# A recurrent attention layer with a gated MLP on one core: a new order table, no tensor arithmetic on GpSimd, and r and v loaded in two transfers without zero rows

## The chip, the cores and the metric

The kernel runs on one core of one Trainium2 chip. A core has five engines that run side by side, each through its own list of instructions in the order in which they were written: TensorE (PE in the profile; PEld are its weight loads), VectorE (DVE), ScalarE (ACT), GpSimd (POOL) and SyncE (SP), which here issues all DMA transfers. They wait for each other through semaphores. The metric is the device time of one execution in microseconds; the number to predict is the median over several runs.

## What is computed

For 32 heads (batch 4 times 8) of size 40, a state of 40x40 is carried through 768 time steps. The outputs of all heads are put side by side, 3072 tokens of 320 numbers, and go through an MLP of width 2048 with the gate h * erf(softplus(h)).

```python
for t in range(S):
    y[:, :, t] = np.einsum('bhd,bhde->bhe', rt, state)
    Sa = np.einsum('bhde,bhe->bhd', state, at)
    state_decay = state * wt[:, :, None, :] - np.einsum('bhd,bhe->bhde', Sa, bt)
    state = state_decay + np.einsum('bhd,bhe->bhde', vt, kt)
...
    h = x @ w_in
    sp = np.maximum(h, 0.0) + np.log1p(np.exp(-np.abs(h)))
    g = h * erf(sp)
    return (g @ w_out).astype(np.float32)
```

## The kernel before

The heads are worked in two groups of 16, the 768 time steps in blocks of 128 (a block is called q here, 12 in all) and these in steps of 32 (48 in all). Names in the profile are those of tiles.

**Before a block's steps.** `prep` scans the decays w (Wt, Pr). `aphase`, once per step, scales k and b (tile bk, L672) and a (tile Ab, L667), sends Ab to the ring Zs by DMA, multiplies them on TensorE (pA, L677), masks the product into Zs (L684), sends part of it to a scratch tensor AD in memory, and transposes bk (L695). `tphase`, once per block, reads AD back as Ti, inverts small triangular matrices there on VectorE (28 short instructions that depend on each other, L724 and L725; called the solve below), sends them out (TD) and back (Tb), transposes them (T, L733) and finishes the inverse with two passes of 128 tiny matmuls on TensorE (L740).

**A step of the chain.** The state MT is copied to Zm; TensorE forms Z (L785) from Zm and Zs; a copy zt; U (L794); a copy us; from us four copies u go into the tile Vu. In the first block these are engine copies out of PSUM; in the other eleven blocks they are four DMA transfers Vu<-Us. Us is transposed (L821) and copied into the tile vt, beside r and v that a DMA brought (vt<-in_rv_e); a product pQ (L830), masked into Vu (L833); and the product my (L841, L845) from Vu, the state and r. From my VectorE adds to the state (MT, L848) and forms the outputs (L852), which leave to a tensor xd. The next step starts from MT.

**The MLP** follows two blocks behind: per block 8 times two products into ph (L1006) and a copy h, then tanh, ln, ln, exp and gelu on ScalarE (L1014), nd, rho, E and G on VectorE (L1039, L1040, L1051, L1052), and the second product into po (L1061). nd, E, bk, Ab, xl (L990, low parts of x) and a few others may run on VectorE or on GpSimd. Weights are loaded and split into high and low parts in the first 140 us (L932 to L963).

**What sets the order.** All operations are recorded in a list with their engines. `Plan.schedule` holds a planner with costs, but it is passed over where two tables, ORDER and ENGINES, fit the list, and they do: ORDER gives the position of each operation, ENGINES its engine by a letter. A -1 in ORDER is a filler, a matmul of 512 columns on constants (L579), that keeps TensorE busy while it waits in the start. All DMA transfers go through SP's queue, one after the other, from the helper `dma` (L576); copies that may run on ScalarE or VectorE go through the helper `copy` (L571 on ScalarE, L573 on VectorE).

## Time and profile before

| | us |
|---|---|
| median of 3 runs | 861.12 (860.7 to 871.73) |
| span of the profiled execution | 855.2 |
| what lies around the span, against the median | 5.9 |
| TensorE busy | 741.9 (87%) |
| VectorE busy | 626.0 (73%) |
| ScalarE busy | 563.6 (66%) |
| GpSimd busy | 145.3 (17%) |

Busy time is the time in which an engine works on an instruction; waiting for semaphores and issuing DMAs is not in it. Fillers count as busy time of TensorE. One execution was profiled; its own time is the span and what the launch puts around it.

### The profile page before, as it was taken

To read this page: it belongs to the slowest core of one execution; us is meant where nothing else is said; L and a number is where in the kernel's file an instruction comes from. 1 tells how busy PE (TensorE), PEld (TensorE's weight loads), DVE (VectorE), ACT (ScalarE), POOL (GpSimd) and SP (SyncE) were. 2 spreads that over 40 slices of the span, in tenths; PEclk is the share of its full clock that TensorE was granted. 3 is DMA by queue.
4 is the path that set the end of the run, shared out by engine and by line. 5 is a ranking of instruction groups with operands and counts; after the bars stand their busy time and mean duration, and the time that the engine had idled before them with its cause. 6 is when DMAs were issued, how large, how long until landed. Compare 5 with 4: busy or idle time off the path is not lost.

```text
span 855.2 us, 32264 instructions
## 1 busy us (share of the span) xinstructions
PE 741.9 (87%) x13794; PEld 572.6 (67%) x13794; DVE 626.0 (73%) x1331; ACT 563.6 (66%) x1055; POOL 145.3 (17%) x124
## 2 busy tenths in 40 slices
PE   0596898798889998989888998899899999899987
PEld 0343546667767777767667776687777777677864
DVE  5588776687767787879687887768688766565764
ACT  5156424677756776865875874685685787567993
POOL 0302111102012012033030100231130240112100
PEclk9998998999999999999999999989999999899998
DMA  7756664665675755556645555746546543512100
GB/s 213 216 155 156 172 157 119 134 135 142 135 169 115 145 139 123 138 121 143 160 122 118 139 130 115 158 109 146 141 112 128 126 112 92 123 39 66 36 16 19
DMA packets 185585, 107.58 MB, mean 126 GB/s; under 512 B 134268, under 2 KB 167804, under 8 KB 185436
## 3 DMA queue, kind: packets, MB, share of 16 engines
q1 hardware_dynamic: 185436, 105.46, 51.8%
q8 instruction: 110, 1.80, 0.9%
q14 instruction: 39, 0.32, 0.1%
HBM read 83.72 MB, written 14.16 MB: 114 GB/s over the span
## 4 chain that ended last, share of the span: by engine, by line
PE 43%; DMA 21%; DVE 14%; SPq 8%; ACT 6%; issue 6%; POOL 1%; DVEq 0%; ACTq 0%; POOLq 0%
PE po L1061 15%; PE ph L1006 10%; SPq L576 8%; DMA Zs<-Ab 3%; PE pA L740 3%; DMA Ti<-AD 3%; PE ph L579 3%; DMA Tb<-TD 2%; PE my L841 2%; PE pQ L830 2%; PE pA L677 2%; DMA bk<-in_kba_e 2%; DMA AD<-Zs 2%; DVE h L1052 2%; PE my L794 2%
## 5 line engine op out<-in xcount | busy, mean ns | idle before, releaser
L1061 PE MATMUL po<-wo,h 128*128 128x320 f32 x768 | 255.1, 459 | 6.1 <-DVE h L1052 5.8
L1061 PEld LDWEIGHTS po<-wo,h 128*128 128x128 f32 x768 | 135.7, 195 | 51.4 <-DVE h L1052 8.7
L1014 ACT ACTIVATE l<-l 128x512 f32<-128x512 f32 x192 | 112.0, 625 | 18.2 <-DVE nd L1039 14.4
L1006 PE MATMUL ph<-xh,wih 128*128 128x256 f32 x384 | 96.1, 332 | 3.4 <-ACT h L571 3.4
L1006 PE MATMUL ph<-xh,wil 128*128 128x256 f32 x384 | 78.0, 285 | 0.0
L1006 PE MATMUL ph<-xl,wih 128*128 128x256 f32 x384 | 77.7, 284 | 0.0
L1052 DVE SCALAR_TENSOR_TENSOR h<-l,h 128x512 f32<-128x512 f32 x96 | 70.3, 739 | 3.0 <-POOL l L1051 2.1
L1040 DVE SCALAR_TENSOR_TENSOR r<-nd,r 128x512 f32<-128x512 f32 x96 | 68.1, 709 | 5.9 <-POOL nd L1039 4.8
L1039 POOL TENSOR_TENSOR nd<-l,r 128x512 f32<-128x512 f32 x27 | 35.7, 1321 | 206.9 <-DVE r L1040 120.4
L1006 PEld LDWEIGHTS ph<-xh,wih 128*128 128x128 f32 x384 | 61.3, 194 | 10.2 <-ACT h L571 4.3
L571 ACT COPY Zm<-MT 40x320 f32<-40x320 f32 x71 | 32.4, 457 | 50.5 <-DVE MT L848 45.6
L579 PE MATMUL ph<-d 104*128 104x512 bf16 x257 | 65.7, 407 | 0.0
L1051 POOL TENSOR_TENSOR l<-l,r 128x512 f32<-128x512 f32 x27 | 38.2, 1419 | 158.6 <-ACT l L1014 85.8
L1006 PEld LDWEIGHTS ph<-xh,wil 128*128 128x128 f32 x384 | 60.6, 194 | 3.9 <-issue 3.9
L1014 ACT ACTIVATE l<-h 128x512 f32<-128x512 f32 x96 | 57.2, 628 | 7.2 <-DVE h L573 6.0
L1006 PEld LDWEIGHTS ph<-xl,wih 128*128 128x128 f32 x384 | 60.2, 192 | 0.0
L1039 DVE TENSOR_TENSOR nd<-l,r 128x512 f32<-128x512 f32 x69 | 49.7, 721 | 11.6 <-ACT r L1014 9.5
L1006 PE MATMUL ph<-xl,wir 128*128 128x256 f32 x192 | 54.9, 286 | 3.8 <-issue 3.7
L841 PE MATMUL my<-Vu,sg 64*40 64x72 f32 x1536 | 48.5, 233 | 8.7 <-DVE h L1052 3.1
L1014 ACT ACTIVATE r<-r 128x512 f32<-128x512 f32 x96 | 55.2, 624 | 0.4
L1014 ACT ACTIVATE r<-l 128x512 f32<-128x512 f32 x96 | 54.2, 619 | 1.5 <-DVE l L1051 1.4
L1006 PE MATMUL ph<-xh,wir 128*128 128x256 f32 x192 | 54.8, 285 | 0.0
(137 smaller groups left out, 1472.5 us busy)
## 6 DMA issues: line engine op xcount, KB each, us to landing
vt<-in_rv_e SPq DMA_DIRECT2D x48, 416.0 KB
bk<-in_kba_e SPq DMA_DIRECT2D x45, 416.0 KB
wo<-in_moe_w_in SPq DMA_DIRECT2D x10, 512.0 KB
h<-in_moe_w_out SPq DMA_DIRECT2D x10, 512.0 KB
Pr<-in_w_e SPq DMA_DIRECT2D x12, 419.7 KB
Rt<-in_r_e SPq DMA_DIRECT2D x48, 104.0 KB
Vu<-in_v_x SPq DMA_DIRECT2D x96, 40.0 KB
Zm<-in_v_s SPq DMA_DIRECT2D x48, 80.0 KB
```

The costliest lines, as they stand in the source:

```text
L571: self.nc.scalar.copy(o, i)
L576: self.P.add(name, "SP", lambda e: self.nc.sync.dma_start(o(), i()), rd, wr, pr, ISSUE.get(name, 0.41))
L579: self.nc.tensor.matmul((self.ph[1], self.pQ)[x], self.d1[:, :128], self.d1[:, :512], start=True, stop=True)
L740: nc.tensor.matmul(pw[js, i], l[js, i], r[js, i], start=True, stop=True)
L841: nc.tensor.matmul(my[h * 64:h * 64 + 40, x, j], sg[xs, j, h], vu[xs, j // 2 * 2 + h, j % 2], start=True, stop=False)
L1006: nc.tensor.matmul(ph[:, j * 256:j * 256 + 256], a[:k, fs], b[:k], start=(m == 0), stop=(m == 7))
L1014: self.P.add(name, "ACT", lambda e: nc.scalar.activation(out=o, in_=i, **kw), rd, wr + ["act"], pr, 0.62)
L1039: P.add("nd", [("DVE", 0.69), ("POOL", 1.28)], lambda e, r=r, l=l, nd=nd: s.eng(e).tensor_tensor(out=nd, in0=l, in1=r, op=ALU.mult), [("l" ...
L1040: P.add("rho", "DVE", lambda e, r=r, nd=nd: nc.vector.scalar_tensor_tensor(out=r, in0=nd, scalar=2 * C4, in1=r, op0=ALU.add, op1=ALU.mult) ...
L1051: P.add("E", [("POOL", 1.28), ("DVE", 0.69)], lambda e: s.eng(e).tensor_tensor(out=l, in0=l, in1=r, op=ALU.mult), [("r", ir)], [("l", il)] ...
L1052: P.add("G", "DVE", lambda e: nc.vector.scalar_tensor_tensor(out=h, in0=l, scalar=-1.0, in1=h, op0=ALU.add, op1=ALU.mult), [("l", il)], [( ...
L1061: nc.tensor.matmul(po, h[:, bs], s.wo[:, f], start=(f == 0), stop=(f == 15))
```

## The change

Both tables are new. The planner is gone; where the tables do not fit, operations now run in the order in which they were recorded (this concerns a fallback path that this input does not enter). No operation of arithmetic may run on GpSimd any more. The list of operations differs in two places: r and v come by two transfers of 40 rows and 3 KB a row, one for each half, instead of one of 104 rows and 4 KB a row, in which rows 40 to 63 and half of r's places were zero; the tile vt is cleared once in the start. And the four copies u read us in all blocks and may run on ScalarE, VectorE or as a DMA: by the new table 106 of the 192 run on ScalarE, 37 on VectorE and 49 as DMAs (before: 11, 5 and 176). A DMA may be issued from GpSimd's queue, but the new table lets SP issue all of them: 828, before 907. The fillers number 124, before 257. The b and k of the block's fourth step in the start go to the ring bk instead of the second vt tile.

```diff
-ORDER = (
-    7, 11, 13, 12, 17, 16, 144, 6, 135, 18, 5, 15, 19, 3, 126, 136, 349, 129, 10, 130, 4, 20, 8, 23, 41, 162, 0, 137, 147, 138, 139, 22, 140, 24, 21,
...
+ORDER = tuple(int(x) for x in """
+20 7 18 22 16 354 355 10 13 9 3 128 8 23 15 11 17 4 131 21 25 0 132 129 6 130 155 27 133 12 134 28 137 146 138 156 26 157 135 30 31 1 32 43 149 35 147 139 55 24 36 38 160 140 37
...
     def dma(self, name, o, i, rd=(), wr=(), pr=0):
-        self.P.add(name, "SP", lambda e: self.nc.sync.dma_start(o(), i()), rd, wr, pr, ISSUE.get(name, 0.41))
+        q = {"SP": self.nc.sync, "POOLQ": self.nc.gpsimd}
+        self.P.add(name, [("SP", ISSUE.get(name, 0.41))] + [("POOLQ", 1.0)] * (name in BULK), lambda e: q[e].dma_start(o(), i()), rd, wr, pr)
...
-            P.add("nd", [("DVE", 0.69), ("POOL", 1.28)], lambda e, r=r, l=l, nd=nd: s.eng(e).tensor_tensor(out=nd, in0=l, in1=r, op=ALU.mult), [("l", il), ("r", ir)], [("nd", i_)], pr)
+            P.add("nd", [("DVE", 0.69)], lambda e, r=r, l=l, nd=nd: s.eng(e).tensor_tensor(out=nd, in0=l, in1=r, op=ALU.mult), [("l", il), ("r", ir)], [("nd", i_)], pr)
...
-        s.dma("rv", lambda: vr, lambda: I["rv_e"][g, ck].rearrange("p (a x) -> p a x", a=NP), wr=[("vt", ivt, 0), ("vt", ivt, 1)], pr=prl)
+        for h in range(2):
+            s.dma("rv", lambda h=h: vr[h * 64:h * 64 + 40, h * 256:h * 256 + 768], lambda h=h: I["rv_e"][g, ck, h], wr=[("vt", ivt, h)], pr=prl)
...
-            if q == 0:
-                P.add("zmu", [("ACT", 0.28), ("DVE", 0.32)], lambda e, uv=uv, js=js: s.copy(e, uv, pz[js]), ["pz"], [("vu", iv, "u", j)], pr)
-            else:
-                s.dma("zu", lambda uv=uv: uv, lambda js=js: uo[js], [("us", iu, "-")], [("vu", iv, "u", j)], pr)
+            q2 = {"SP": nc.sync.dma_start, "ACT": nc.scalar.copy, "DVE": nc.vector.tensor_copy}
+            P.add("zu", [("ACT", 0.28), ("DVE", 0.25), ("SP", 0.6)], lambda e, uv=uv, js=js: q2[e](uv, uo[js]), [("us", iu, "-")], [("vu", iv, "u", j)], pr)
```

The new tables move instructions everywhere; three places show it. First TensorE's list in the second chain step of the start, from Z (out of Zm and Zs) to U (out of zt and Tb) and what follows it. Before:

```order
L785 MATMUL my<-Zm_77,Zs_69 32x40 x16
L579 LDWEIGHTS d_113
L579 MATMUL ph_159<-d_113 128x512
L579 LDWEIGHTS d_113
L579 MATMUL ph_159<-d_113 128x512
L579 LDWEIGHTS d_113
L579 MATMUL ph_159<-d_113 128x512
L794 MATMUL my<-zt_109,Tb_83 32x40 x16
L677 MATMUL pA<-Ab_76,bk_99 64x2x32 x8
```

Now, where L592 is Z, L617 the transpose of MT, L601 U, L626 the transpose of Us, L387 a filler and L483 the product pA:

```order
L592 MATMUL my<-Zm_77,Zs_69 32x40 x16
L617 MATMUL pQ<-ident,MT 104x104 x4
L601 MATMUL my<-zt_109,Tb_83 32x40 x16
L626 MATMUL pQ<-ident,Us_85 104x128 x2
L387 LDWEIGHTS d_113
L387 MATMUL ph_159<-d_113 128x512
L483 MATMUL pA<-Ab_76,bk_99 64x2x32 x8
```

The three fillers between Z and U gave way to the transpose of the state, and the transpose of Us now follows U directly.

Second VectorE's list in the middle of the first solve (L724 and L725 on the tile Ti; L932 to L942 prepare weights). Before:

```order
L724 TENSOR_TENSOR tmp_106<-Ti 128x54
L942 TENSOR_TENSOR wil_127<-l_132,wih_125 128x512
L942 TENSOR_TENSOR wil_126<-l_136,wih_124 128x512
L937 TENSOR_TENSOR l_136<-l_135,r_138 128x512
L933 SCALAR_TENSOR_TENSOR r_139<-wo,r_139 128x512
L725 TENSOR_TENSOR Ti<-Ti,tmp_106 128x6x9
L724 TENSOR_TENSOR tmp_106<-Ti 128x56
L725 TENSOR_TENSOR Ti<-Ti,tmp_106 128x7x8
L724 TENSOR_TENSOR tmp_106<-Ti 128x56
L725 TENSOR_TENSOR Ti<-Ti,tmp_106 128x8x7
L937 TENSOR_TENSOR l_132<-l_131,r_139 128x512
```

Now, with the solve at L530 and L531 and the weights at L737 to L742:

```order
L531 TENSOR_TENSOR Ti<-Ti,tmp_106 128x4x11
L742 TENSOR_TENSOR l_132<-l_131,r_139 128x512
L530 TENSOR_TENSOR tmp_106<-Ti 128x50
L531 TENSOR_TENSOR Ti<-Ti,tmp_106 128x5x10
L530 TENSOR_TENSOR tmp_106<-Ti 128x54
L531 TENSOR_TENSOR Ti<-Ti,tmp_106 128x6x9
L737 TENSOR_SCALAR r_137<-wo 128x512
L530 TENSOR_TENSOR tmp_106<-Ti 128x56
L531 TENSOR_TENSOR Ti<-Ti,tmp_106 128x7x8
L530 TENSOR_TENSOR tmp_106<-Ti 128x56
L531 TENSOR_TENSOR Ti<-Ti,tmp_106 128x8x7
```

Before, 11 instructions of other work stand between the first and the last of the 28; now three do (two of 512 columns with two inputs, one with one).

Third SP's list around the sixth chain step. Before:

```order
L576 DMA Vu_78<-in_v_x 32x8x40
L576 DMA Vu_79<-Us_85 32x4x40 x2
L576 DMA AD_118<-Zs_70 32x8x32
L576 DMA Zm_77<-in_v_s 32x640
L576 DMA Vu_79<-Us_85 32x4x40
L576 DMA Rt_82<-in_r_e 104x256
L576 DMA Vu_78<-in_v_x 32x8x40
L576 DMA Vu_79<-Us_85 32x4x40
L576 DMA AD_118<-Zs_70 32x8x32
```

Now, with L611 for a copy u as a DMA and L384 for all others:

```order
L384 DMA vt_107<-in_rv_e 40x768
L384 DMA Zm_77<-in_v_s 32x640
L611 DMA Vu_79<-Us_85 32x4x40
L384 DMA Vu_78<-in_v_x 32x8x40
L384 DMA AD_118<-Zs_70 32x8x32
L384 DMA Vu_79<-in_v_x 32x8x40
L384 DMA AD_118<-Zs_70 32x8x32
L384 DMA Rt_82<-in_r_e 104x256
```

Of the four Vu<-Us of that step one is left in SP's list, and vt<-in_rv_e stands there twice per step.

## Rows read from the trace of the kernel before

**Rows 1.** Busy time by engine in four stretches between marks of the program: the wait for the first inverse, the first four chain steps (to the fourth MT), the 43 steps up to the 47th MT, and the end. Columns: the stretch and its length, busy time (and instructions) of PE, PEld, DVE, ACT and POOL, the granted clock of TensorE, the DMA share, GB/s.

```profile
39.70:75.60 35.90, 28.03 (x119) 12.07 (x118) 28.32 (x65) 19.13 (x37) 5.37 (x4) 0.96 0.58 143
75.60:131.30 55.70, 49.43 (x1026) 28.04 (x1026) 40.45 (x89) 23.08 (x53) 6.51 (x6) 0.96 0.71 177
131.30:777.10 645.80, 585.10 (x12066) 472.36 (x12066) 486.57 (x1052) 448.79 (x846) 115.44 (x95) 0.97 0.55 127
777.10:855.20 78.10, 69.69 (x471) 52.56 (x471) 47.17 (x85) 58.47 (x95) 9.11 (x6) 0.95 0.08 25
```

**Rows 2.** The chain of work that ended last: shares of the whole span by engine, and shares of the stretch from 131.3 to 777.1 us by line. SPq is SP issuing, a DMA's time runs from its issue to its landing.

```profile
PE 43%; DMA 21%; DVE 14%; SPq 8%; ACT 6%; issue 6%; POOL 1%; DVEq 0%; ACTq 0%; POOLq 0%
...
by line: PE po L1061 15.6%; PE ph L1006 12.4%; SPq L576 9.4%; issue 6.2%; PE pA L740 4.0%; DMA Zs<-Ab 3.8%; DMA Ti<-AD 3.5%; DMA Tb<-TD 3.3%; PE my L841 2.6%; PE pA L677 2.3%; PE pQ L830 2.2%; DMA AD<-Zs 2.0%; PE my L794 2.0%; DVE h L1052 1
```

**Rows 3.** Timeline of TensorE around a wait in the middle of the span: start and length in us, and in brackets the idle time before. The same transpose of MT (L812) stands behind the wait and 14 us later.

```profile
555.04 0.37 PE L1006 MATMUL ph<-xl,wir 128*128 128x256 f32 x1 [3.67 <-issue]
...
555.64 0.90 PE L812 MATMUL pQ<-ident,MT 104*104 104x104 f32 x4
...
570.13 0.56 PE L812 MATMUL pQ<-ident,MT 104*104 104x104 f32 x4
```

**Rows 4.** The fillers: busy time of PE and PEld by L579 alone in the first two stretches of rows 1, and two pieces of the chain of work in order of time (start, length).

```profile
39.70:75.60 35.90, 27.99 (x116) 12.04 (x116) 0.96 0.58 143
75.60:131.30 55.70, 32.09 (x126) 11.37 (x126) 0.96 0.71 177
...
107.13 1.30 PE ph L579 x6
...
108.88 1.30 PE ph L579 x6
```

**Rows 5.** Timeline of VectorE: first and last instruction of the first solve, then of the second, with pieces out of its middle.

```profile
54.15 0.17 DVE L724 TENSOR_TENSOR tmp<-Ti 128x14 f32<-128x14 f32 x1
...
66.43 0.17 DVE L725 TENSOR_TENSOR Ti<-Ti,tmp 128x14 f32<-128x14 f32 x1
...
110.12 0.17 DVE L724 TENSOR_TENSOR tmp<-Ti 128x14 f32<-128x14 f32 x1
...
113.01 0.20 DVE L725 TENSOR_TENSOR Ti<-Ti,tmp 128x44 f32<-128x44 f32 x1
113.25 0.21 DVE L724 TENSOR_TENSOR tmp<-Ti 128x50 f32<-128x50 f32 x1
...
113.51 1.25 POOL L672 TENSOR_TENSOR bk<-bk,Wt 104x512 f32<-104x512 f32 x1 [1.50 <-DMA bk<-in_kba_e]
113.74 1.09 DVE L724 TENSOR_TENSOR tmp<-Ti 128x54 f32<-128x54 f32 x1
...
119.25 0.17 DVE L725 TENSOR_TENSOR Ti<-Ti,tmp 128x14 f32<-128x14 f32 x1
```

**Rows 6.** Operations of VectorE beside GpSimd. Of two lines first the group (count | busy us, mean ns | idle before it), then the same instructions' shortest, median and longest time in ns; last GpSimd's share of a third line.

```profile
L1052 DVE SCALAR_TENSOR_TENSOR h<-l,h 128x512 f32<-128x512 f32 x96 | 70.3, 739 | 3.0 <-POOL l L1051 2.1
L1052 DVE SCALAR_TENSOR_TENSOR h<-l,h x96: 644/685/2432, 180.7 to 844.9; 128x512 f32<-128x512 f32 x96
L667 DVE TENSOR_TENSOR Ab<-bk,Pr 104x512 f32<-104x512 f32 x36 | 30.1, 835 | 14.9 <-DMA Zs<-Ab 11.7 <-DMA Vu<-Us 3.2
L667 DVE TENSOR_TENSOR Ab<-bk,Pr x36: 676/691/2492, 21.4 to 696.5; 104x512 f32<-104x512 f32 x36
L1039 POOL TENSOR_TENSOR nd<-l,r x27: 1264/1285/1787, 202.1 to 785.8; 128x512 f32<-128x512 f32 x27
```

**Rows 7.** SP's issues of three transfers (shortest, median and longest time of one issue in ns), the size of two of them, and the queue's packets, MB and share of the 16 engines.

```profile
L576 SPq DMA_DIRECT2D Vu<-Us x176: 585/605/1823, 141.2 to 784.4; - x176
L576 SPq DMA_DIRECT2D vt<-in_rv_e x48: 307/480/2112, 30.6 to 768.2; - x48
vt<-in_rv_e SPq DMA_DIRECT2D x48, 416.0 KB
Vu<-Us SPq DMA_DIRECT2D x176, 20.0 KB
q1 hardware_dynamic: 185436, 105.46, 51.8%
```

**Rows 8.** Copies: those of u out of PSUM in the first block, on ScalarE and on VectorE, and one of h on VectorE (ns as above).

```profile
L571 ACT COPY Vu<-my x11: 282/283/285, 86.7 to 124.0; 32x160 f32<-32x160 f32 x11
L573 DVE COPY Vu<-my x5: 318/329/331, 85.1 to 123.6; 32x160 f32<-32x160 f32 x5
L573 DVE COPY h<-ph x20: 651/684/693, 150.0 to 826.3; 128x512 f32<-128x512 f32 x20
```

**Rows 9.** Who TensorE waited for (us in total, times, longest us), and one wait of U for the copy zt in the timeline.

```profile
PE pA L740 <- DVE T L733: 13.4, 6, 7.9
PE pA L677 <- DVE Ab L667: 8.4, 4, 2.9
PE po L1061 <- DVE h L1052: 5.8, 5, 2.7
PE my L785 <- DMA Zm<-in_v_s: 4.6, 5, 1.5
PE my L841 <- DMA Vu<-Us: 1.6, 2, 1.2
119.87 0.37 PEld L794 LDWEIGHTS my<-zt,Tb 32*32 32x32 f32 x32 [0.42 <-ACT zt L571]
```

More of the change, by code (lines that the diff above doesn't have):

```diff
@@ L295, in add @@
             self.rd[k] = []
-        every, one = alts, self.only.get(name + self.tag, self.only.get(name))
-        alts = [x for x in every if x[0] == one] or every
-        self.ops.append(dict(name=name, tag=self.tag, alts=alts, all=every, fn=fn, deps=deps, pr=pr, banks=[k for k in rd if k in self.BANKS], uses=[k for k in self.SPARE if k in rd or k in wr]))
+        self.ops.append(dict(name=name, tag=self.tag, alts=alts, fn=fn, deps=deps, keys=set(rd) | set(wr)))
         return i
     def schedule(self):
-        ops = self.ops
@@ L303, in schedule @@
-        n = len(ops)
-        if len(self.engines) == n and sorted(x for x in self.order if x >= 0) == list(range(n)):
-            for o, e in zip(ops, self.engines):
-                o["eng"] = dict(P="PE", A="ACT", V="DVE", G="POOL", S="SP")[e]
-            out = []
-            for x in self.order:
-                if x < 0:
-                    ops.append(dict(name="warm", eng="PE", fn=lambda e, x=-1 - x: self.filler(x)))
-                    x = len(ops) - 1
-                out.append(x)
-            return out
@@ L314, in schedule @@
-        succ = [[] for _ in range(n)]
-        left = [0] * n
-        for i, o in enumerate(ops):
-            left[i] = len(o["deps"])
-            for d, raw in sorted(o["deps"]):
-                succ[d].append((i, raw))
-        ready_at = [0.0] * n
-        free = {e: 0.0 for e in self.HOP}
-        ticks = {}
-        queue = lock = 0.0
-        only = [o["alts"][0][0] if len(o["alts"]) == 1 else "" for o in ops]
-        bank = {k: ("", 0.0) for k in self.BANKS}
-        uses = {k: sum(k in o["uses"] for o in ops) for k in self.SPARE}
@@ L420, in schedule @@
-        assert done == n, (done, n)
-        self.total = max(o["end"] for o in ops)
-        return sorted(range(len(ops)), key=lambda i: (start[i], i))
+        ops, n = self.ops, len(self.ops)
+        if len(self.engines) != n or sorted(x for x in self.order if x >= 0) != list(range(n)):
+            for o in ops:
+                o["eng"] = o["alts"][0][0]
+            return list(range(n))
+        for o, e in zip(ops, self.engines):
+            o["eng"] = CODE[e]
+        out = []
+        for x in self.order:
+            if x < 0:
+                ops.append(dict(name="warm", eng="PE", fn=lambda e, x=-1 - x: self.filler(x)))
+                x = len(ops) - 1
+            out.append(x)
@@ L425, in restride @@
+        return out
 def restride(ap, dim, step):
@@ L462, in host @@
     o["r_e"] = stk(re).reshape(NG, 24, 104, NP * 32)
[L463 to L466 removed]
+    rs, vs = [el(x)[:, :, :, :, [pair(n) for n in range(NP)]] for x in (r, v)]
+    vu = np.zeros((NG, 24, 2, 40, NP, 2, 32), np.float32)
+    vu[..., 0, :] = vs
+    rv = np.zeros((NG, 24, 2, 40, 3 * NP * 32), np.float32)
+    for h in range(2):
+        rv[:, :, h, :, (256, 0)[h]:(768, 512)[h]] = vu[:, :, h].reshape(NG, 24, 40, NP * 64)
+        rv[:, :, h, :, (0, 512)[h]:(256, 768)[h]] = rs[:, :, h].reshape(NG, 24, 40, NP * 32)
+    o["rv_e"] = rv
     vs = v.reshape(NG, NB, 4, 2, 24, 32, 40).transpose(0, 4, 5, 1, 2, 3, 6)
@@ L500, in __init__ @@
         K = self.K
-        self.P = Plan(K.get("po", {}), self.warm, K.get("warm", 4.0), order=ORDER, engines=ENGINES)
+        self.P = Plan(self.warm, ORDER, ENGINES)
         pool = lambda n, **k: ctx.enter_context(tc.tile_pool(name=n, bufs=1, **k))
@@ L1158, in build @@
             mlp(q)
-        if "prs" in K:
-            for o, x in zip(N.P.ops, K["prs"]):
-                o["pr"] = x
         order = N.P.schedule()
```

222 lines of the change are left out of this document (54 added, 168 removed), and 303 rows, old and new, of the table ORDER.

## The prediction

> **What bounds the kernel now.** I read the busy time by stretch first [rows 1]. In the 43 chain steps that fill most of the span, 645.8 us, TensorE is busy for 585.1 us and idle for 60.7; VectorE is busy for 486.6 us (75%), ScalarE for 448.8 (69%). So TensorE bounds this stretch, at 91%, and an order can win there at most the idle time and what the clock loses. The four chain steps of the start are different: of TensorE's 49.4 busy us in 55.7, 32.1 are fillers [rows 1, 4], so 17.3 us are work, and the stretch goes at the speed of a chain of short steps across all engines. Next I read the chain of work that ended last [rows 2]: TensorE has 43% of the span, DMA 21%, VectorE 14%, SP's issuing 8%, ScalarE 6%, GpSimd 1%. Last the clock [rows 3]: behind an idle time of 3.67 us the same transpose takes 0.90 us that takes 0.56 us 14 us later; that is work at the lower of the two levels, 1.2 instead of 2.4 GHz. In the 43 steps the granted clock is 0.97, which at 585.1 busy us is 17.6 us lost for 60.7 us of idle time, 0.29 us for each us. Saved idle time brings that back too.
>
> **The change part by part.** I make the sum against the profiled execution's 855.2 us; the median is 5.9 us above it.
>
> *The start.* Three things. (a) The first solve runs from 54.15 to 66.60, 12.45 us, with 11 other instructions in it [rows 5]. Undisturbed, one of its 28 instructions follows the other after 0.24 us (113.01 to 113.25), 6.7 us in all; the three that are left in it cost at most 0.69 us each [rows 6], so it takes 8.8 us: minus 3.7. The weight work pushed behind it is late instead, but nothing of the MLP is asked of TensorE before the fifth chain step. (b) The second solve takes 9.3 us (110.12 to 119.42), with a piece that took 1.09 us beside a GpSimd instruction [rows 5]. Now only one update of MT stands in it: 6.7 plus about 0.5, minus 2.1. (c) From the first to the fourth step the order has 26 fillers, before 90. A filler takes 0.217 us (six in 1.30) and lies on the chain there [rows 4]; 64 of them are 13.9 us. Bounds: nothing, if the second inverse (its DMAs to memory and back) is what the next block waits for anyway, and 13.9. I take 12, near the upper end, because the rows show fillers on the chain itself. Together minus 18; at the lower bound of (c), minus 6.
>
> *Copies u.* 127 of 176 transfers Vu<-Us go, and ScalarE gets 95 copies more, VectorE 32 more. On SP an issue took 0.605 us [rows 7]: 76.8 us less, against 48 more issues of rv at 0.48, 23.0. SP's list shrinks from 907 issues to 828, 9%. In the 43 steps SP's issuing has 9.4% of the chain, 60.7 us [rows 2]; 9% of that is minus 5.3. Bounds: nothing, and 53.8 (all of it on the chain); the small share on the chain speaks for the lower end. TensorE's direct waits for these transfers sum to only 1.6 us [rows 9]; 127 of 176 of that is minus 1.2.
>
> *rv in two transfers.* Each step moves 2 x 40 x 3 KB = 240 KB instead of 416 [rows 7]: 48 x 176 KB, 8.4 MB, and with the copies u (127 x 20 KB, 2.5 MB) 10.9 of 105.5 MB, 10.4%. Nobody on the chain waits much for rv itself; what gains is what queues behind it. The four small transfers on the round trip to memory and into Zs (Zs<-Ab, Ti<-AD, Tb<-TD, AD<-Zs) have 12.6% of the chain, 81.4 us [rows 2]; 10.4% of it is minus 8.5. Bounds: nothing (their own latency), and 15.4, if all of rv, a fifth of the bytes, had stood in front of them. I take the share of the bytes. The Trainium skill speaks against this edit: "DMA: Bandwidth & Descriptors", Rules for kernel authors, says that two transfers to disjoint halves of the partitions do not pay, since they serialize on the same engines. Its section on why a DMA increments its semaphore by 16 adds that a transfer uses as many engines, up to 16, as divide its rows: 13 for 104 rows, 10 for 40. An estimate by that page: 24 KB per engine and step instead of 32, a quarter less, so that the term would be minus 5.9. No row shows the engines of one transfer.
>
> *GpSimd's arithmetic.* 115 operations move: 94 of 512 columns at 0.69 us on VectorE [rows 6], 64.9 us, and 21 smaller ones, up to 14 more; I take 73 together. In return VectorE's own operations are no longer stretched: L1052 has a mean of 739 ns against a median of 685, L667 835 against 691 [rows 6], 5.2 us each. VectorE hands 12 copies of h at 0.684 [rows 8] and some 32 smaller ones, at no less than 0.27, to ScalarE, minus 16.8, and takes 32 copies u at up to 0.329, plus 10.5. Net plus 56 us, and ScalarE gets plus 47 (95 x 0.283 [rows 8] and the copies). What hides this is idle time: in the 43 steps VectorE has 159 us free and ScalarE 197 [rows 1]. By their shares of the chain, 14% and 6% [rows 2], it costs plus 7.9 and plus 2.8. On the other side an operation that waited for GpSimd took 1.285 us there [rows 6]; GpSimd's 1% of the chain, 8.6 us, about halves: minus 4.0. Net plus 6.7; bounds minus 14 (all stretching and GpSimd's share on the chain, the new load hidden) and plus 56.
>
> *The rest of the order.* Between Z and U TensorE needs about 0.65 us of other work to cover the copy zt; with nothing between them it idles for 0.42 [rows 9]. By the order that cover is short in 18 of the last 44 steps before and in 4 now, but between U and the transpose of Us it is short more often now (7 against 2). I put nothing down for it.
>
> *Sum.* -18 - 5.3 - 1.2 - 8.5 + 6.7 = -26.3; the 15 us of terms that shorten waits in the 43 steps bring 0.29 x 15 = 4.4 us of clock back. 855.2 - 30.7 = 824.5 us, and with 5.9 us around it 830 us, 3.6% less.
>
> **Rivals.**
>
> *The waits shrink much more.* Both tables steer every wait; if the new one halves the idle time of the 43 steps (minus 30.4, with the clock minus 8.8) beside the start's minus 18, it is 855.2 - 57.2 + 5.9 = 804 us. For it: the largest waits are few and long (L740 for T 13.4 us in 6, L677 for Ab 8.4 in 4 [rows 9]), the kind that an order can remove. Against it: VectorE and ScalarE have less room than before.
>
> *The waits only change their place.* The fillers go, but the second inverse sets the start; SP's and DMA's savings end at engines that are fuller. Then the solves' 5.8 us are left: 855 us. For it: several engines are three quarters full.
>
> *TensorE runs cold in the start.* With 133 fillers fewer it idles instead, and the 17.3 us of work of the four steps run at 1.2 GHz, twice as long: 830 + 17 = 847 us. For it: rows 3. Against it: 46 fillers of that stretch remain, between the longest waits. The Trainium skill, "TensorE: Matmul & The Clock Gate", section on HAM oscillation, says the same, that bursts between idle gaps start cold; by that rule the trace agrees for gaps of some us.
>
> *VectorE becomes the bound, and it gets slower.* The place is the MLP's nd, rho, E and G: those that ran beside VectorE now stand in its one list, ahead of the masks and MT updates for which TensorE waits. Each us on the path costs 1.29 with the clock. Without the start's gain, the savings of SP, DMA and clock (19) stand against it; it is slower by over 2% once more than 28 of the 56 us lie on the path, and with three quarters of them it is 861 - 19 + 54 = 896 us. For it: G already holds TensorE up (5.8 us [rows 9]). Against it: 159 us free.
>
> **How the numbers follow.** Forecast 0.50, its own range 815 to 844; waits much shorter 0.20; waits change place 0.14; cold start 0.06; VectorE bound 0.10. A measurement of this kernel can tell about 2%, 17 us, from no change: below 844 is faster, above 878 slower. Faster 0.70 (the first two), same 0.20 (the next two), slower 0.10. The range for 8 times in 10 goes from 798, below the first rival, to 862, which takes in the two middle ones and leaves out the last.
>
> **What would show it.** In the changed profile the fourth MT update should stand near 113 us (now 131.3) and the first solve take under 9.5 us; the 43 steps 632 to 638 us, with TensorE idle under 50; SP's share of the chain under 8% of them; VectorE's mean for L1052's line within 10 ns of its median; VectorE's busy time near 680 us, ScalarE's near 610. The prediction is wrong if VectorE appears as the releaser of most of TensorE's waits, if the copies of h or tanh start later behind ScalarE's new copies, if the first four steps show matmuls of double length, or if the second inverse waits for its DMAs as long as before.

## The result, and the profile after

The changed kernel takes 784.09 us in the median (779.93 to 791.56, 4 runs), the kernel before 860.91 us beside it; the ratio is 0.9143, interval 0.9075 to 0.9211. That is 8.6% less where 3.6% were forecast, and below the forecast range; it is also below 798 us, the lower end of the range for 8 times in 10. The profiled execution spans 780.8 us (before 855.2), 74.4 us less. Its own time, 782.75 us, is 2.0 us above its span; so the 5.9 us that the forecast put around the span were mostly the distance of the profiled execution from the median.

By the marks of [rows 1], the fourth MT update stands at 110.0 us (131.3 before), the 47th at 702.5 (777.1), and the end takes 78.3 us (78.1). So the start gave 21.3 us, the 43 steps 53.3 and the end nothing. The busy time by stretch, from the last product of the first block's pA to the first inverse, to the fourth MT, to the 47th, and to the end; columns as in [rows 1]:

```profile
33.30:57.90 24.60, 11.34 (x50) 4.67 (x48) 22.34 (x61) 13.27 (x26) 0.00 (x0) 0.72 0.89 234
57.90:110.00 52.10, 41.75 (x945) 26.96 (x946) 37.20 (x88) 28.81 (x67) 0.00 (x0) 0.74 0.63 159
110.00:702.50 592.50, 571.60 (x12056) 470.69 (x12055) 506.62 (x1153) 492.79 (x967) 0.00 (x0) 0.99 0.51 123
702.50:780.80 78.30, 68.16 (x474) 52.99 (x473) 50.62 (x88) 56.65 (x93) 0.00 (x0) 0.94 0.08 24
```

In the 43 steps TensorE is idle for 592.5 - 571.6 = 20.9 us, before 60.7: 39.8 us less. Its busy time fell by 13.5 us. Of these 3.3 are fillers (5.6 us in 15 before, 2.3 us in 8 now); the other 10.2 came with a granted clock of 0.99 instead of 0.97, which is 0.26 us for each us of idle time saved, where the forecast had 0.29. VectorE is now 86% busy there and ScalarE 83%, and still TensorE waits less. In the start the clock is only 0.72 to 0.74 (0.96 before); what such a clock costs in the old order is shown by old_fewfill below. The chain that ended last, by engine over the span and by line over the 43 steps (L866 and L811 are the MLP's products, L1061 and L1006 before):

```profile
PE 75%; ACT 7%; DVE 7%; DMA 4%; issue 4%; SPq 1%; DVEq 0%; ACTq 0%
...
by line: PE po L866 30.3%; PE ph L811 25.3%; PE pA L546 5.1%; PE my L646 4.4%; PE pQ L635 4.3%; PE pA L483 3.8%; PE my L601 3.2%; issue 3.0%; PE my L592 2.9%; PE pQ L617 2.5%; PE pA L501 2.3%; PE my L650 1.8%; PE pQ L626 1.5%; ACT l L819 1.
```

Beside [rows 2], TensorE went from 43 to 75%, DMA from 21 to 4%, SP's issuing from 8 to 1%: the chain is now nearly TensorE's list alone. Whom TensorE waited for in the 43 steps (us in total, times, longest), before and after. The sums of [rows 9] are those of the whole span, so the lines of before are given for the same stretch:

```profile
PE pA L740 <- issue: 7.4, 4, 2.6
PE pA L740 <- DVE T L733: 5.5, 5, 2.2
PE pA L677 <- DVE Ab L667: 4.7, 2, 2.9
PE my L785 <- DMA Zm<-in_v_s: 4.6, 5, 1.5
PE my L794 <- issue: 4.0, 2, 3.2
```

```profile
PE pA L546 <- issue: 4.9, 3, 2.2
PE my L601 <- issue: 2.9, 3, 1.3
PE ph L811 <- issue: 2.2, 1, 2.2
PE pA L483 <- DVE nd L844: 2.0, 1, 2.0
PE pA L483 <- issue: 1.7, 2, 0.9
PE pQ L626 <- ACT Sm L378: 1.4, 1, 1.4
PE my L646 <- DMA Vu<-Us: 1.2, 1, 1.2
```

The waits for T, Ab and Zm are gone. Of the 20.9 us that are left, 11.7 are "issue", time in which TensorE waited for nothing that the profile shows; what it is stays open. Where the idle time of the 43 steps went I summed from TensorE's timeline, step by step, between the products of the chain (us over 43 steps: length of the way, idle in it; UT is the transpose of Us, and what is missing from the 60.7 and 20.9 us lies within the products):

```
             MT to Z     Z to U      U to UT    UT to pQ   pQ to my   my to MT
before     124.0 12.4   93.9 17.6   90.0 2.4   81.6 7.6   74.2 14.3   36.3 0.2
after      106.3  2.4  120.9 11.1   66.0 2.2   57.4 0.1   67.4  0.2   33.0 0.0
```

The saving is no single wait: about 10, 6, 8 and 14 us in four places. The new order also spreads TensorE's other work anew: the way from Z to U is 27 us longer, the two ways from U to pQ are 48 us shorter.

The start, VectorE's timeline (first and last instruction of each solve, to [rows 5]):

```profile
40.56 0.17 DVE L530 TENSOR_TENSOR tmp<-Ti 128x14 f32<-128x14 f32 x1 [1.19 <-DMA Ti<-AD]
...
48.09 0.19 DVE L531 TENSOR_TENSOR Ti<-Ti,tmp 128x14 f32<-128x14 f32 x1
...
92.51 0.16 DVE L530 TENSOR_TENSOR tmp<-Ti 128x14 f32<-128x14 f32 x1
...
100.74 0.18 DVE L531 TENSOR_TENSOR Ti<-Ti,tmp 128x14 f32<-128x14 f32 x1
```

The first solve takes 7.72 us (12.45 before), but above all it starts 13.6 us earlier; the second takes 8.41 (9.3). The first inverse begins at 57.9 us (75.6 before), so 17.7 of the start's 21.3 us stand there already. SP's timeline shows the order of the first loads. Before, then after (start, length of the issue; Pr<-in_w_e is the w of the block, bk<-in_kba_e k, b and a of the first step):

```profile
0.75 1.34 SPq L576 DMA_DIRECT2D wo<-in_moe_w_in  x3
...
2.63 0.62 SPq L576 DMA_DIRECT2D Pr<-in_w_e  x1
...
7.71 0.34 SPq L576 DMA_DIRECT2D bk<-in_kba_e  x1
```

```profile
1.20 0.44 SPq L384 DMA_DIRECT2D Pr<-in_w_e  x1
...
3.66 0.53 SPq L384 DMA_DIRECT2D bk<-in_kba_e  x1
```

The first block's w now has one weight transfer ahead of it, not three. In the chain before, in order of time, four bulk transfers fill 33.9 of the first 43.8 us, the last of them the w of the second block, which VectorE scans just ahead of the solve:

```profile
1.66 6.03 DMA wo<-in_moe_w_in
7.71 10.58 DMA bk<-in_kba_e
...
26.45 6.98 DMA wo<-in_moe_w_in
33.49 10.32 DMA Pr<-in_w_e
...
46.38 2.81 DMA Ti<-AD
...
50.23 2.27 DVE Pr L636 x2
```

After, VectorE scans the second w (L444) while the solve's data is still on its round trip, whose last piece in the chain is the transfer of 5.70 us:

```profile
35.33 2.35 DVE L444 TENSOR_TENSOR_SCAN Pr<-Pr,d 104x516 f32<-104x516 f32 x2
```

```profile
34.76 5.70 DMA Ti<-AD
```

So the solve's data lands at 40.5 us instead of 49.2, 8.7 us earlier; the other 4.9 us are VectorE's work between the landing and the solve, which no longer stands there. The order does this, not the engines and not rv: among the runs below the first solve starts at 42.7 us in new_order_old_code (new order, old engines) and at 52.6 us in old_order (old order, new engines). That the loads are what counts in it is read from the chain; no run moves the loads alone.

### The profile page after: what moved, and what is told of

Its sections match the earlier page's. It is cut to its first block, busy times and chain, and to the rows that moved or that the text cites. A ratio compares the mean times of both kernels' runs of the same rounds, so it can differ in the third digit from the quotient of the medians.

```text
span 780.8 us, 31875 instructions
## 1 busy us (share of the span) xinstructions
PE 708.3 (91%) x13661; PEld 564.2 (72%) x13661; DVE 645.3 (83%) x1434; ACT 614.1 (79%) x1194; POOL 4.0 (1%) x12
## 3 DMA queue, kind: packets, MB, share of 16 engines
q1 hardware_dynamic: 166332, 94.20, 48.6%
## 4 chain that ended last, share of the span: by engine, by line
PE 75%; ACT 7%; DVE 7%; DMA 4%; issue 4%; SPq 1%; DVEq 0%; ACTq 0%
PE po L866 26%; PE ph L811 20%; PE pA L546 4%; PE pQ L635 4%; PE my L646 4%; PE pA L483 3%; PE my L601 3%; PE my L592 2%; PE pA L501 2%; PE pQ L617 2%; PE ph L387 2%; ACT r L819 2%; PE my L650 2%; ACT l L819 1%; PE pQ L626 1%
## 5 line engine op out<-in xcount | busy, mean ns | idle before, releaser
L866 PE MATMUL po<-wo,h 128*128 128x320 f32 x768 | 269.7, 460 | 4.9 <-DVE ob L380 3.9
L866 PEld LDWEIGHTS po<-wo,h 128*128 128x128 f32 x768 | 127.3, 192 | 35.4 <-DVE ob L380 4.9
L811 PE MATMUL ph<-xh,wih 128*128 128x256 f32 x384 | 118.1, 389 | 0.5 <-DVE h L380 0.4
L811 PEld LDWEIGHTS ph<-xh,wih 128*128 128x128 f32 x384 | 70.9, 191 | 27.2 <-DVE h L380 0.6
L844 DVE TENSOR_TENSOR nd<-l,r 128x512 f32<-128x512 f32 x96 | 65.9, 687 | 17.0 <-ACT r L819 12.2
L811 PE MATMUL ph<-xl,wih 128*128 128x256 f32 x384 | 77.2, 283 | 2.2 <-issue 2.2
L811 PE MATMUL ph<-xh,wil 128*128 128x256 f32 x384 | 77.0, 282 | 0.0
L856 DVE TENSOR_TENSOR l<-l,r 128x512 f32<-128x512 f32 x96 | 64.6, 681 | 0.9 <-ACT l L819 0.5
L857 DVE SCALAR_TENSOR_TENSOR h<-l,h 128x512 f32<-128x512 f32 x96 | 65.0, 683 | 0.4
L811 PEld LDWEIGHTS ph<-xl,wih 128*128 128x128 f32 x384 | 59.3, 190 | 2.4 <-issue 2.4
L811 PEld LDWEIGHTS ph<-xh,wil 128*128 128x128 f32 x384 | 59.7, 190 | 0.0
L378 ACT COPY h<-ph 128x512 f32<-128x512 f32 x88 | 50.8, 581 | 11.0 <-PE ph L811 10.4
L490 DVE TENSOR_TENSOR Zs<-pA,tri 64x256 f32<-64x256 f32 x96 | 40.6, 423 | 22.7 <-PE pA L483 19.3
L811 PE MATMUL ph<-xl,wir 128*128 128x256 f32 x192 | 54.4, 283 | 0.0
L811 PE MATMUL ph<-xh,wir 128*128 128x256 f32 x192 | 54.1, 282 | 0.0
L483 PE MATMUL pA<-Ab,bk 104*64 104x64 f32 x720 | 33.3, 236 | 19.9 <-DVE bk L478 15.3
```

The source lines that it names most:

```text
L378: self.nc.scalar.copy(o, i)
L483: nc.tensor.matmul(pa[i % 2 * 64:i % 2 * 64 + 64, i // 4, i // 2 % 2], bk[:, i].rearrange("p a b -> p (a b)"), ab[:, :, i], start=True, st ...
L490: P.add("Am", "DVE", lambda e, x=x, xs=xs: nc.vector.tensor_tensor(out=zx[64:128, x], in0=pz[xs], in1=s.tri[xs, None, :].to_broadcast([64, ...
L811: nc.tensor.matmul(ph[:, j * 256:j * 256 + 256], a[:k, fs], b[:k], start=(m == 0), stop=(m == 7))
L844: P.add("nd", [("DVE", 0.69)], lambda e, r=r, l=l, nd=nd: s.eng(e).tensor_tensor(out=nd, in0=l, in1=r, op=ALU.mult), [("l", il), ("r", ir) ...
L856: P.add("E", [("DVE", 0.69)], lambda e: s.eng(e).tensor_tensor(out=l, in0=l, in1=r, op=ALU.mult), [("r", ir)], [("l", il)], pr)
```

## Experiments

Each run is named by its label: `old_` runs start from the old order, `new_` runs from the new one. Ratios are to the kernel before, with their intervals; one percent is 8.6 us. Where an edit is a table, the diff names the table, since its numbers tell nothing.

**Order against engines.** Two theories: **O**, the new order itself shortens the waits; **E**, the waits went because GpSimd's slow pieces and the DMA copies of u left the chain.

```diff
 old_order (the changed code)
-order new, engines new, rv in two transfers
+order old, engines new, rv in two transfers
 new_order_old_code (the code before)
-order old, engines old, rv in one transfer
+order new, engines old, rv in one transfer
```

> The order of the kernel before (its 257 fillers too) with everything else of the change: no arithmetic on GpSimd, u copied by engines where the new table does so, rv in two transfers; three operations come a few places later, since one tile changed. Theory O (the new order itself shortens the waits): the time stays near the kernel before, 840 to 875 us, and the 43 steps keep over 45 us of TensorE idle. Theory E (the waits went because GpSimd's slow pieces and the DMA copies of u left the chain): 800 to 825 us, idle under 35 us there. The forecast's own terms for engines, SP and bytes (-5.3 - 1.2 - 8.5 + 6.7) give about 850 us.

> The code, engines and transfers of the kernel before (GpSimd's arithmetic, u by DMA, rv in one transfer) in the new order, with its 124 fillers. Theory O: most of the gain is there, 785 to 810 us. Theory E: 830 to 865 us, since GpSimd's 1.2 us pieces and the four DMAs of u stand again between the chain's steps.

Measured: old_order 904.99 us, ratio 1.0559 (1.0454 to 1.0663); new_order_old_code 951.92 us, 1.1021 (1.0891 to 1.1151). Both halves of the change are slower than the kernel before; together they are 8.6% faster. Theory O and theory E fall both as stated, since both times lie above all that either gave. In old_order TensorE waits for engines all over its 43 steps, here the four largest:

```profile
PE pQ L628 <- ACT Sm L380: 8.7, 8, 3.8
PE my L603 <- DVE Tb L555: 7.8, 4, 6.5
PE my L648 <- ACT Vu L613: 5.9, 6, 2.3
PE po L868 <- DVE h L859: 5.9, 5, 3.1
```

Then one part of the engines at a time is put back in the changed kernel, GpSimd's 115 operations or the 127 DMA copies. One place of each, on VectorE and on ScalarE:

```diff
 new_pool, VectorE's list
 L638 TENSOR_TENSOR Vu_78<-pQ,tri 128x8x32
-L844 TENSOR_TENSOR nd_141<-l_136,r_138 128x512
 new_udma, ScalarE's list
 L378 COPY vt_107<-pQ 104x8x32
-L611 COPY Vu_78<-Us_85 32x4x40
 L378 COPY h<-ph_159 128x512
```

> The changed kernel with only the 115 operations of tensor arithmetic back on GpSimd. Theory O: within 8 us of the changed kernel (776 to 792 us). Theory E with GpSimd as its cause: 800 us or more, VectorE's L857 line with a mean 40 ns or more above its median, and waits of TensorE for POOL or for DVE pieces stretched beside it.

> The changed kernel with only the copies u back on DMA where the kernel before had them so (127 copies move). Theory O: within 8 us of the changed kernel (776 to 792 us). Theory E with the DMA copies as its cause: 800 us or more, with waits of my for Vu<-Us of over 15 us in the 43 steps (1.2 us in the changed kernel) and SP's issuing over 5% of the chain.

Measured: new_pool 793.58 us, 0.9227 (0.9121 to 0.9333), its interval overlapping that of the changed kernel; GpSimd's arithmetic costs 0.8%, some 7 us, or nothing, and the time lies between what the two theories gave. new_udma 886.26 us, 1.0292 (1.0204 to 1.0379): the DMA copies cost 11.5% of the time before, some 99 us, in the new order, as theory E had it with the copies as its cause. TensorE's largest wait in its 43 steps (from an execution with a span of 896.1 us):

```profile
PE my L646 <- DMA Vu<-Us: 53.7, 32, 4.3
```

The new order leaves 5.1 us between the copy us and my (mean over the 43 steps, from the timelines; 6.4 before). The last of the four DMA issues ends 3.9 us after us in the kernel before and 4.8 us after it in new_udma, and the data has to land after that.

**One part alone in the old order.** Theory **P**: parts and order belong together. Theory **S**: the parts add up.

```diff
 old_nopool, VectorE's list
+L969 TENSOR_TENSOR nd_141<-l_136,r_138 128x512
 L970 SCALAR_TENSOR_TENSOR r_138<-nd_141,r_138 128x512
 old_u (engines old, but for the 127 copies u)
-                s.dma("zu", lambda uv=uv: uv, lambda js=js: uo[js], [("us", iu, "-")], [("vu", iv, "u", j)], pr)
+                q2 = {"SP": nc.sync.dma_start, "ACT": nc.scalar.copy, "DVE": nc.vector.tensor_copy}
+                P.add("zu", "SP", lambda e, uv=uv, js=js: q2[e](uv, uo[js]), [("us", iu, "-")], [("vu", iv, "u", j)], pr, 0.41)
 old_rv (the changed code)
-order new, engines new
+order old, engines old
 old_fewfill, TensorE's list, 64 times between the first and the fourth MT
-LDWEIGHTS d_113
-MATMUL ph_159<-d_113 128x512
```

> The kernel before with one part of the change alone: its 115 operations of arithmetic on GpSimd run on VectorE, at the same places of the list. The forecast put this part at plus 6.7 us (bounds minus 14 and plus 56), 847 to 917 us. Theory P (parts and order belong together: an order made for one set of engines loses with another): slower, 870 to 900 us, since VectorE's list now holds 0.69 us pieces where the order had left them to another engine. Theory S (the parts add up): within 10 us of 861 us, as the reverse cost the changed kernel 9.5 us.

> The kernel before with one part alone: the 127 copies u that the new table gives to engines run there (92 on ScalarE, 35 on VectorE), in the old order, in the eleven blocks that had DMAs. Theory P: the old order holds at least 5.4 us of TensorE's other work between U and my in every step, enough for the DMAs, so copies that land earlier free nobody: 850 to 880 us, and U to my stays above 6.3 us per step. Theory S (the copies by themselves are the gain of the new order, 100 us there): 800 us or less. The forecast's terms for it (-5.3 - 1.2 and a part of the bytes) give about 852.

> The kernel before with one part alone: r and v in two transfers of 40 rows and no zero rows (the b and k of the fourth step of the first block go to the ring bk, as in the changed kernel; three operations come a few places later). The forecast gave the bytes minus 8.5 us and SP's 48 further issues at most plus 23 us. Theory P and theory S both expect little: 845 to 865 us; over 870 us would mean that two transfers cost SP's queue more than the bytes save.

> The kernel before without 64 of the 90 fillers between its first and its fourth MT update, thinned evenly. The forecast's step (c): minus 12 us, the fourth MT near 119 us (131.3). If the fillers only fill what TensorE waits for anyway: the fourth MT within 3 us of 131.3 and 855 to 865 us. If the start runs cold for want of them and that is on the chain: the fourth MT after 135 us.

Measured: old_nopool 863.47 us, 1.0011 (0.9969 to 1.0054): nothing, as theory S had it. old_u 879.26, 1.0185 (1.0081 to 1.029): slower, as theory P had it. old_rv 847.38, 0.9823 (0.973 to 0.9915): 15 us. old_fewfill 863.42, 1.0016 (0.9973 to 1.0059): nothing; its stretch to the fourth MT:

```profile
75.60:131.40 55.80, 46.23 (x850) 27.16 (x841) 38.09 (x88) 21.19 (x50) 6.06 (x5) 0.69 0.67 168
```

The fourth MT stands at 131.4 us, as before, with the clock at 0.69 instead of 0.96. So neither the fillers nor the clock set the start's time in the old order.

The parts do not add up to old_order. GpSimd, u and rv together come to plus 0.2%; old_order, with all engines of the change and rv, is 5.6% slower than the kernel before. The 46 us between are the parts' effect on each other, or that of the 47 copies which the table also moves from VectorE to ScalarE (16 into Sm, 12 into h, 7 into vt and others; six operations go the other way). No run moves these alone.

In old_u the waits of my for copies show what went wrong:

```profile
PE my L772 <- ACT Vu L737: 10.2, 7, 3.3
...
PE my L772 <- DVE Vu L737: 5.0, 5, 1.7
```

The last engine copy of a step ended 4.2 us after us (mean, from the timelines), since it stood in its engine's list behind other work.

**rv, the start, and the length of the way from U to my, in either order.** Theory **C**: the way from U to my, 6.84 us per step before and 5.57 after (the three ways between them in the table, and the two products that stand there), is itself the gain, since what does not stand there covers other waits.

```diff
 new_rv_one
-        for h in range(2):
-            s.dma("rv", lambda h=h: vr[h * 64:h * 64 + 40, h * 256:h * 256 + 768], lambda h=h: I["rv_e"][g, ck, h], wr=[("vt", ivt, h)], pr=prl)
+        P.add("rv", "SP", lambda e: nc.sync.dma_start(vr, I["rv_e"][g, ck]), (), [("vt", ivt, 0), ("vt", ivt, 1)], prl)
...
 new_start
-order and engines new
+order and engines new up to the fourth MT, old behind it
 new_late and new_udma_late, TensorE's list, one step
+L811 MATMUL ph_159<-xh_0_145,wih_124 128x256
...
 L646 MATMUL my<-Vu_78,sg_95 40x72 x4
...
-L811 MATMUL ph_159<-xh_0_145,wih_124 128x256
```

> The changed kernel with r and v again in one transfer of 104 rows and 4 KB a row (416 KB), at the place of the first of the two. The same edit in the other direction made the kernel before 1.8% faster, 15 us. If the bytes are what counts, the changed kernel loses about as much: 795 to 803 us. If the gain came from where the old order put the transfer: 780 to 790 us.

> The changed kernel's list up to its fourth MT update, with its engines, and behind it the old order with the old engines (GpSimd's arithmetic, u by DMA), rv in two transfers throughout. It is to be held against the run with the old order and only the new rv (847 us). If the start's gain is separate from the rest: about 21 us less, 820 to 832 us, the fourth MT near 110 us and the 43 steps as long as there (634 us). If the rest gives it back, 840 us or more.

> The changed kernel, engines and copies untouched, but in 35 of the 43 steps the product my is moved behind further matmuls of TensorE, so that about 7 us of other work lie between U and my, as in the kernel before (5.6 us in the mean now); the state's update and what needs it come right behind it. Nothing else moves. Theory C (the short way from U to my is itself the gain, because the work it frees covers other waits): 800 us or more, since the state then stands with less cover behind my. If TensorE's list has slack there: 780 to 792 us.

> The same list as in the run before it, with the 127 copies u as DMAs where the kernel before had them so (886 us with my where the new order has it). If the DMAs cost only by their latency, in an order that leaves too little between U and my, the waits of my for Vu<-Us fall from 54 us to under 15 and the time to within 15 us of the run before it. If SP's issuing of them is what costs, it stays above 860 us, with the waits moved to other transfers.

Measured: new_rv_one 799.0 us, 0.9341 (0.9278 to 0.9403), 2.0% of the time before more than the changed kernel. new_start 834.8, 0.9766 (0.9697 to 0.9835): 0.6% below old_rv by the ratios, within the intervals, and between the two times that were expected; its fourth MT stands at 111.3 us (131.1 in old_rv), but the 43 steps behind it take 639.9 us (634.4). new_late 822.59, 0.957 (0.9487 to 0.9653): 37 us slower than the changed kernel, as theory C had it, with TensorE waiting for the state's copy (ACT Zm, 9.1 us). new_udma_late 888.0, 1.033 (1.024 to 1.042): beside new_late, which has the same list, the DMA copies cost 7.6% of the time before, some 65 us, where they cost 99 beside the changed kernel, and the wait for Vu<-Us falls from 53.7 to 23.5 us. More room between us and my takes off part of their price; their latency is not the whole of it.

Where rv can gain is read from the chain in order of time. The rows are those of the kernel before, then those of new_rv_one; neither old_rv nor the changed kernel has such a piece among the longest of its 43 steps:

```profile
150.95 5.55 DMA vt<-in_rv_e
...
398.50 5.05 DMA vt<-in_rv_e
```

```profile
431.76 5.83 DMA vt<-in_rv_e
...
654.56 6.05 DMA vt<-in_rv_e
```

Two pieces of 5 to 6 us, 10.6 and 11.9 us; with the forecast's 0.29 us of clock for each us, 13.7 and 15.3. That is an estimate, and the two pairs of runs show 15 and 17, each known to some 8 us. In old_rv two pieces of bk<-in_kba_e stand on the chain (6.1 and 4.7 us); the run with fewer bytes for these, new_kba below, is in the new order, where none does.

**The way from U to my, the other direction.** Theory **L**: old_u lost by the place of its copies alone.

```diff
 old_u_early, ScalarE's list
 L501 COPY Us_85<-my 128x4x40
+L737 COPY Vu_79<-Us_85 32x4x40 x2
 L893 CAST wir<-l_132 64x512
...
-L737 COPY Vu_79<-Us_85 32x4x40 x2
 old_u_early_my, TensorE's list, one step (old_my_early the same without the copies, new_early in the new order)
-L937 MATMUL ph_158<-xh_0_145,wih_124 128x256
...
 MATMUL my<-Vu,sg
...
+L937 MATMUL ph_158<-xh_0_145,wih_124 128x256
```

> The kernel before with the 127 copies u on ScalarE and VectorE as in the run with this part alone (879 us), but now each copy stands in its engine's list right behind the copy us that it reads, not at the place where the DMA had been. Theory L (those copies lost because they stood behind other work: the last landed 4.2 us after us in the mean): the last copy lands under 2 us after us, the waits of my for Vu (17 us) are gone and the time falls to 845 to 862 us. If the load of the two engines is what costs: 870 us or more.

> The run before it, and in each of the 43 steps the last one to three products of the MLP that stood between U and my (about 1.8 us of TensorE's work) are moved behind my; U to my is then about as short as in the changed kernel (5.6 us, 6.8 before). Theory C (a short way from U to my is the gain of the new order, and the engine copies allow it): 815 to 840 us. If the length of that way has no effect of its own and the searched places of everything else are the gain: within 10 us of the run before it, or slower.

> The same products moved behind my in the kernel before with its DMA copies of u. They need 3.9 us of issuing in the mean and then land, so theory C expects TensorE to wait for Vu<-Us, 25 us or more over the 43 steps (1.6 before), and 870 us or more. If the list has slack there: 850 to 865 us.

> The changed kernel with the way from U to my shortened further, by one or two MLP products a step (1.2 us in the mean), which go behind my. Making it longer by about as much cost 38 us. Theory C taken strictly (shorter is better): 765 to 780 us. If any shift away from the searched places costs: 795 us or more; if TensorE, 96% busy in the 43 steps, has no more waits to give: within 6 us of 784.

Measured: old_u_early 866.09 us, 1.0003 (0.9951 to 1.0056): the last copy ends 1.1 us after us, the waits of my for copies are gone, and the copies cost nothing and gain nothing in the old order. Theory L holds for the loss; the median is 4 us above the range that it gave. Right behind us is not where the changed kernel has its copies: there the last one of a step ends 3.2 us after us (mean), and my does not wait for one, since the order has it stand later still. old_u_early_my 923.06, 1.0709 (1.0627 to 1.079); old_my_early 911.72, 1.0594 (1.0519 to 1.0668); new_early 805.97, 0.9343 (0.9279 to 0.9407). Theory C, taken as shorter is better, falls in the new order: moving my forward costs 61, 51 and 17 us. Only in new_early is the way shorter than in the changed kernel (5.0 us for 5.6). In the two old runs it is still 6.6 and 6.2 us long, since TensorE idles 1.9 and 1.6 us in it, so there a way of 5.6 us was not reached and theory C not put to the test. TensorE's largest waits in old_u_early_my, old_my_early and new_early:

```profile
PE my L772 <- DVE Vu L764: 25.7, 24, 2.9
```

```profile
PE my L771 <- DVE Vu L763: 23.4, 20, 3.6
PE my L771 <- DMA Vu<-Us: 7.4, 5, 3.0
```

```profile
PE my L646 <- DVE Vu L638: 9.5, 16, 1.2
```

The wait is for the mask of pQ into Vu, not for u: from us a second way leads to my, over the transpose, vt, pQ and the mask, and it too needs TensorE's other work beside it. Even with my pulled forward, only 7.4 us of waits fall to the DMAs in old_my_early, not the 25 expected. From us to my there are 5.7 us there, as in new_udma, where the waits were 53.7; but the last of the four issues ends 3.7 us after us, not 4.8, so SP's list in the new order, made for fewer of these transfers, has a part in their price.

**Does it add up, and are rv's 15 us bytes?**

```diff
 new_kba
-        s.dma("kba", lambda: kb[:, :4 * NP * 32], lambda: s.I["kba_e"][g, ck], wr=[kk, kk + ("a",)], pr=pr)
+        def kba(e):
+            if q == 0:
+                s.nc.sync.dma_start(kb[:, :4 * NP * 32], s.I["kba_f"][c])
+            else:
+                for h in range(2):
+                    s.nc.sync.dma_start(kb[h * 64:h * 64 + 40, h * 256:h * 256 + 768], s.I["kba_e"][g, ck, h])
+        P.add("kba", "SP", kba, (), [kk, kk + ("a",)], pr)
...
 old_start (the changed code)
-order and engines new
+order and engines old up to the fourth MT, new behind it
```

> The changed kernel with the same edit for k, b and a as the change made for r and v: after the first block, two transfers of 40 rows and 3 KB a row in place of one of 104 rows and 4 KB (240 KB for 416 in 44 of 48 steps); the places left out keep the zeros of the first block's transfers, which stay whole. Order and engines untouched. If what counts is the bytes (rv's edit gave 15 us for 8.4 MB in either order): 7.7 MB less, 768 to 778 us, a version better than both kernels. If rv's edit gained by its place in SP's list: 780 to 790 us; if the 44 further issues disturb the searched order: 790 us or more.

> The complement of the run with the new start: the old order and engines up to the fourth MT update, and behind it the new order with the new engines; rv in two transfers throughout. If start and rest add up: 784 plus 13 to 21, 797 to 805 us, with the 43 steps near 592 us. If the new rest needs its own start (transfers and weights in another state): 815 us or more.

Measured: new_kba 786.03 us, 0.9147 (0.9094 to 0.92), the changed kernel's time, though 7.9 MB less went through the queue (86.28 MB, 94.20). In this order nobody waits for these transfers: fewer bytes and 44 further issues together change nothing. No run beats the changed kernel. old_start 797.09, 0.9278 (0.9235 to 0.9321). The 43 steps of old_rv, new_start and old_start:

```profile
131.10:765.50 634.40, 582.32 (x12068) 471.70 (x12067) 488.13 (x1052) 449.82 (x846) 117.04 (x95) 0.98 0.49 118
```

```profile
111.30:751.20 639.90, 584.44 (x12067) 473.54 (x12067) 485.73 (x1051) 446.67 (x841) 114.42 (x95) 0.97 0.49 118
```

```profile
131.20:719.00 587.80, 569.30 (x12055) 468.50 (x12054) 506.75 (x1152) 492.73 (x967) 0.00 (x0) 0.99 0.51 123
```

The rest of the list keeps its gain behind the old start. So the ratios give two ways from one kernel to the other. From 1 to 0.9823 by rv (15 us), to 0.9278 by order and engines behind the fourth MT (47 us), to 0.9143 by the start (12 us); or, with the start before the rest, 15, 5 and 54 us. Each step is known to some 7 to 10 us.

## Why the prediction was wrong

**The step that failed** is the last of the parts: "The rest of the order: ... I put nothing down for it." The order and the engines of the 43 steps, taken together, are worth 47 to 54 us of the 74, and neither half gains alone: the new engines in the old order cost 7.4% of the time before against old_rv (old_order, 1.0559, against 0.9823), and the DMA copies in the new order 11.5%. The two places that I looked at for this term, from Z to U and from U to the transpose of Us, idle 6.5 and 0.2 us less; most of the saving is before Z and between the transpose of Us and my, where I did not look. I costed each part by its share of the chain of the kernel before, as if the rest stood still. But such a list had no place to give where it was tried: moving my by a microsecond or so per step costs 17 to 61 us in either direction. The bound was in the text, 60.7 us of idle time and 17.6 of clock; the first rival took half of the idle time and came to 804. It was the right mechanism, and two thirds of the idle time went. Its argument rested in part on a wait outside the 43 steps: of the 13.4 us for T in [rows 9], 7.9 are one wait of the start.

**The start** was forecast at 18 us; 21.3 are seen at the fourth MT, and 12 are left at the end by one pair of runs and 5 by the other. The 43 steps behind the new start are some 5 us longer in both (592.5 to 587.8, 639.9 to 634.4), which is no more than two executions of one kernel differ by. Its parts were wrong. The first solve's 3.7 measured 4.7 and the second's 2.1 measured 0.9, but the fillers' 12 measured nothing (old_fewfill): fillers on the chain are there because TensorE waits with or without them. In their place stands the earlier start of the first solve, 13.6 us, which I did not cost; the chain before shows four bulk transfers ahead of it.

**rv** was forecast at 8.5, by its share of the bytes (with the copies' bytes), with the sentence that nobody on the chain waits much for rv itself. It measured 15 us (7 to 23) and 17 in the two orders. The total of the bytes does not explain it, as new_kba shows in the new order; two pieces of the chain were waits for rv. TensorE's direct waits hid them, since SP, GpSimd and ScalarE waited for rv in the kernel before (4.5, 5.5 and 4.0 us). The Trainium skill ("DMA: Bandwidth & Descriptors", Rules for kernel authors), by which two transfers to disjoint halves do not pay, did not hold against this change: two smaller ones gained for rv and were neutral for k, b and a. Since the bytes fell in both cases, no run shows the splitting alone.

**Copies u.** SP's 5.3 and the waits' 1.2 measured nothing in the old order, once the copies stood early (old_u_early), and a loss of 16 where they stood late. In the new order they are needed (new_udma).

**GpSimd** was forecast at plus 6.7 with bounds minus 14 and plus 56; it measured 0.1% (-0.3 to 0.5) in the old order and some 7 us or nothing in its removal's favour in the new one. VectorE's busy time rose by 37.4 us in old_nopool (663.4 from 626.0), not by the 73 put on it: the moved operations take 73.3 us there, but VectorE's own, no longer beside GpSimd's, take 28.6 less, of which I had priced two lines at 10. L1052's line, L857 now, shows the step itself right:

```profile
L857 DVE SCALAR_TENSOR_TENSOR h<-l,h x96: 649/683/693, 154.5 to 769.7; 128x512 f32<-128x512 f32 x96
```

**The signs.** The fourth MT near 113 (110.0), the first solve under 9.5 us, idle under 50, SP's share under 8% and ScalarE near 610 (614.1) came as named; the 43 steps (592.5 for 632 to 638) and VectorE (645.3 for 680) did not. The rival of a cold TensorE came in its premise, a clock of 0.74; in the old order such a clock cost nothing (old_fewfill), in the new one no run shows its price apart. The one of VectorE as the bound did not come, nor did the one of waits that change their place.

**What stays open.** Which places of the new order carry the 47 us is not settled. The idle time went from four places at once, each shift of my away from its place cost time, and no rule was found in the table that a reader could apply elsewhere. What the 47 copies between VectorE and ScalarE do alone is open too, and so is the price of the DMA copies beyond the waits for them.

## What to carry to other kernels

When order and engine assignment change together, neither half need have a price of its own. Bound the time from below by taking off the idle time and the lost clock of the bounding engine, and give a good part of that bound its own chance, instead of adding up shares of the old chain. Read the chain in order of time, not only by sums: two waits of 5 us for a bulk transfer, and bulk transfers ahead of the first dependent chain, are what a smaller or later transfer can remove, while 7.9 MB off the chain were worth nothing here. A copy that moves from a DMA to an engine needs a place in that engine's list early enough for its reader: at the DMA's old place it cost 16 us, right behind its source nothing, and neither gained by itself.

## What the hardware showed unexpectedly

The copies u cost other times out of SBUF than [rows 8] had out of PSUM, 0.323 us on ScalarE (0.283) and 0.234 on VectorE (0.329):

```profile
L611 ACT COPY Vu<-Us x106: 320/323/327, 72.6 to 706.9; 32x160 f32<-32x160 f32 x106
...
L611 DVE COPY Vu<-Us x37: 232/234/242, 80.7 to 709.6; 32x160 f32<-32x160 f32 x37
```

The Trainium skill ("Perfetto Trace Analysis", Optimizing Scalar/DVE Operations) gives overheads by which a ScalarE operation costs about 42 ns more on SBUF than on PSUM and a VectorE operation about 65 ns less. The trace agrees for ScalarE (40 ns) and in sign for VectorE (95 ns).
